# Batch 1's first heads split in the opening, loads and splits dated one by one, an output piece on ScalarE's queue

## The chip, the core and the metric

One NeuronCore of a Trainium2 chip runs the whole program. Its engines are TensorE (PE, matrix multiplies into PSUM), VectorE (DVE), ScalarE (ACT), GpSimd (POOL) and SyncE (SP, which here only issues DMAs); each works through its own list of instructions in order and waits on semaphores. 16 DMA engines move data; SP and ScalarE issue to hardware queues (q1 and q10 in the profile), GpSimd to a software queue (q0), which also casts on the way. The metric is the device time of one execution in microseconds, lower is better.

## What is computed

Clustered attention, then a two-layer network over its output:

```python
# q, k, v: 4 batches x 8 heads x 768 rows x 64, f32; centroids: 8 x 16 x 64
q_assign = argmax(einsum('bhsd,hcd->bhsc', q_n, c_n))      # nearest of 16 centroids, rows normalised
k_assign = argmax(einsum('bhsd,hcd->bhsc', k_n, c_n))
mask = q_assign[:, :, :, None] == k_assign[:, :, None, :]
scores = where(mask, q @ k.T / 8, -1e9)
attn = softmax(scores)
x = (attn @ v)  as 3072 x 512                               # rows of a batch, heads side by side
h = x @ w_in                                                # 512 x 2048
out = (h * sigmoid(h)) @ w_out                              # 2048 x 512
```

## The kernel before

**A head's inputs.** A *job* is what is loaded, split and transposed together: for batches 1 to 3 the job `h8` to `h31` of one head holds its six 128-row tiles of q and six of k (`raw`, f32). The head is *split* into two f16 parts, `hi` (L124, on ScalarE, GpSimd or DVE) and `lo` (L137, on DVE), and transposed as a whole: for `h8` and up by a DMA transposition that SP issues (`xpose`, L144), for batch 0 on PE. The transposed tile `ab` has 128 rows: the 64 of a head dimension and room for the one-hot *codes* of the nearest centroid. For these, twelve small matmuls with the centroids (`logits_n`, L178, tile `psN`), three DVE steps (sum, maximum, comparison), a matmul that turns the one-hot tile (`cd_mm`, L249), an eviction with scale (`cd_ev`, L258) and a DMA on SP into rows 64 to 79 of `ab` (L269). For batches 2 and 3 the codes go another way, by a DMA transposition and a DMA of GpSimd (L239, L243). With codes in both operands one matmul gives the score and a bonus where the clusters agree, which stands for the mask.

**Score units.** A unit is one head, one half of the query rows (384) and two key tiles: two matmuls into a double bank (`qk_mm`, L352, tile `pS`), then one exp on ScalarE (`exp`, L365, tile `P`). There are 192 units, 24 for each half of a batch. Six units later a *weighted sum* (`pv`, L373, 36 matmuls, tile `pO`) takes the P tiles of two heads, DVE normalises, and the result is transposed into `xt`, on PE or by DMA (`xn_d`, L416).

**The network.** A *first-layer piece* (`unit_a`, L437, tile `ph`) is four matmuls, a tanh on ScalarE and a gate on DVE (L452), which also frees the bank; 16 pieces make one half batch. The *second layer* (`part_b`, L464, tile `po`) takes four matmuls of w_out at a time; for most row tiles of batches 1 to 3 pairs of tiles are done by `Pair` (L519) with seven half products in place of eight, for which DVE builds sums of rows and differences of w_out (`tw_piece`, L496).

**Weights.** GpSimd issues eight pieces of w_in (`w0` to `w7`) and four of w_out (`w8` to `w11`, 512 KB each in f16) in `w_load` (L601). The last two wait for exps of units 22 and 23: a small copy out of the P tile (`pace`, L603) stands ahead of each on GpSimd.

**What sets the order.** The whole order is written into the program when it is built, nothing is decided on the chip. The opening is a list of words by hand (`plan`, L777): `r9` loads h9, `v3` casts a value tile, `qk11` and `ex11` are a unit's matmuls and exp, `e6.3` is a first-layer piece in bank 3, `w10` a weight piece; it ends after the exp of unit 26 and eight first-layer pieces. From there a planner takes over (L810 to L1230): it keeps an estimated clock for each engine, a backlog for the DMA engines (`lands`, L823), and picks step by step the next instruction for the engine that is free first. PE chooses among score units (held to a pace, L1148 to L1152), logits, weighted sums, first-layer pieces and second-layer pieces; seven-step turns (`turn`) alternate between the last two. Splits, loads and value casts of a head start at *dates*, which are unit numbers: before, a formula gives head by head the date of its split (L924), and load, values and cast stand at fixed distances from it (L927 to L931).

Buffers bind as well: raw tiles have eight places (`raw_tag`, L110), hl tiles four and later three, value loads five, P sixteen. A tile that takes a place waits on the chip until its last reader is done, whatever the planner thought.

**The end.** The last pair's last quarter product is made in two halves (`c21_last`, L593), one evicted on ScalarE, one on DVE, and both are sent by SP.

Of the kernel before, what the change touches and what calls it, by code (L numbers as in the profile page):

```python
# [34 lines left out]
def kernel(  # L35
# [74 lines left out]
    def raw_tag(n):  # L110
        return f"raw{n % 8 if n < EARLY else 5 + n % 3}"

    def load(job, eng=nc.sync):
        n = len(raws)
        raw = mp.tile([128, 12, D], f32, name="raw", tag=raw_tag(n), bufs=1)
        for dst, ap in job.srcs:
            o = raw[:, dst, :]
            if len(ap.shape) == 2:
                eng.dma_start(o.rearrange("p n d -> p (n d)"), ap)
# [245 lines left out]
    def exp(u):  # L365
        P = mp.tile([128, 2, HALF], f16, name="P", bufs=16)
        nc.scalar.activation(out=P, in_=pst.pop(u)[:, :, 0:HALF], func=AF.Exp, bias=0.0, scale=ESC)  # L367
        Ps[units[u]] = P

# [141 lines left out]
    def keep(b, n):  # L511
        if b not in cps:
            cps[b] = [mp.tile([128, HK, 128], f16, name="cp", tag=f"ab{10 + m}", bufs=1) for m in range(2)]
        nc.sync.dma_start(cps[b][n], gts[b, 0][:, n * HK : n * HK + HK, ts(NM - 1, 128)])
# [4 lines left out]
    class Pair:  # L519
# [73 lines left out]
        def c21_last(self, part):  # L593
            x = slice(part * HD // 2, part * HD // 2 + HD // 2)
            if part:
                nc.vector.tensor_copy(self.ot2[:, x], self.A[:, x])
            else:
                nc.scalar.activation(out=self.ot2[:, x], in_=self.A[:, x], func=AF.Copy, bias=0.0, scale=1.0)
            nc.sync.dma_start(self.rows()[:, 0, x], self.ot2[:, x])
# [82 lines left out]
    def first(op, n, eng, banks):  # L682
# [48 lines left out]
        elif op == "w":  # L731
            w_load(n, {10: 22, 11: 23}.get(n))
# [23 lines left out]
        elif op == "xt":  # L756
            xpose(xj)
# [29 lines left out]
        qk23 px3.3 pt1.1 pe1.D ex23 pt2.0 xc1 py3 qk24 pe2.D w7 r9 xe1.A r10 nm3 ex24 qk25 a0.1 pt3.0 w8 qk26 a1.2  # L787
        pe3.D ex25 w9 e0 e1 w10 e6.3 r11 e4.0 ex26 e2.1 e3.2 e5.3 w11 e7.0
# [21 lines left out]
    clock = dict.fromkeys(("PE", "ACT", "DVE", "POOL", "SP"), 0.0)  # L810
    lanes = {e: [] for e in clock}
# [3 lines left out]
    PACE, LEAST, GAIN = 1.40, 17, .03  # L815
    HOLD = 6
    MARGIN = 0.3
    EARLY_T = 72


    moves_end = 11
# [34 lines left out]
    code_at, tensor_todo, after_unit = {}, [], {}  # L856

    def chain(job, b):
        def split(t):
            if job.name not in loaded:  # L860
                waiting[job.name] = split
                return
            t = max(t, loaded[job.name] + 0.4)
            either(t, 0.5, 0.72, lambda e: hi(job, "act" if e == "A" else None), lambda t: add("DVE", t, 0.9, lambda: lo(job), turned, 1.5), 1.5)

        def turned(t):
            u = last_use.get(place[job.name] - 12, 0)
# [4 lines left out]
            add("SP", t, 1.5, lambda: xpose(job), lambda t: tensor_todo.append((lands(t, 2.45) + (5.0 if b == 3 else 2.2 if b == 2 else 1.8), 0.35, lambda: logits_1(job), sums)), 0.0 if b == 1 else 3.0)  # L872
# [21 lines left out]

        return split
# [4 lines left out]
    loaded, waiting, values_at = {}, {}, {}  # L900
# [4 lines left out]

    def got(job, t):
        loaded[job.name] = lands(t - 0.25, 1.31)
        if job.name in waiting:
            waiting.pop(job.name)(t)

# [5 lines left out]
    def cast(i, t):  # L916
        if i not in values_at:
            waiting[i] = lambda t: cast(i, t)
        else:
            add("POOL", max(t, values_at[i] + 0.4), 0.6, lambda: cast_v(i))  # L920

    for i in range(H, B * H):
        b, h = divmod(i, H)
        p = int((32 + 3.2 * h, 67+5.0*h, 106+5.2*h)[b - 1]) | 1  # L924
        job = jobs[i]
        if i > H + 3:
            date(max(FIRST, p - (8 + min(h, 4) if b == 1 else 16)), lambda t, job=job: add("SP", t, 1.05, lambda: load(job), lambda t: got(job, t), 3.0))  # L927
        if i >= H + 2:
            date(p - (6 if b == 1 else 9), lambda t, i=i, b=b: add("POOL", t, 0.6, lambda: load_v(i, nc.gpsimd), lambda t: got_v(i, t)) if b >= 2 else add("SP", t, 0.7, lambda: load_v(i), lambda t: got_v(i, t)))
        date(p - (3 if b == 1 else 6), chain(job, b))  # L930
        date(p, lambda t, i=i: cast(i, t))  # L931
# [27 lines left out]
    kinds = {(b, c): [0, 1, 2] for b in range(B) for c in range(2)}  # L959
    for b, c in kinds:  # L960
        if b >= 1:
            kinds[b, c] = ["p", 2]
        if b >= 2:
            kinds[b, c] = ["x", "p"] if c else ["p"]
# [41 lines left out]
    def new_pair(b, c, kind):  # L1006
        key = b, c, kind
        at.setdefault(key, {})
        t = (1 if b >= 2 else 0) if kind == "p" and c else 0
        if kind == "x":  # L1010
            r2 = (lambda h: cps[b][h]) if b in cps else tokens(b, 0, NM - 1)
            pairs[key] = Pair(kind, b, tokens(b, 1, 0), r2, NM - 1, SG[kind])
        else:
            pairs[key] = Pair(kind, b, tokens(b, c, t + 1), tokens(b, c, t), c * NM + t, SG[kind], key == LAST)
# [10 lines left out]
        if not users[kind] or "over" in at[users[kind][-1]]:  # L1025
            tell(key, "turn", 0.0)
        users[kind].append(key)
        def over(t):
            add("DVE", t + 0.2, 0.69, pr.c12, sent)
            tell(key, "over", t)  # L1030
            n = users[kind].index(key) + 1
            if n < len(users[kind]):
                tell(users[kind][n], "turn", t)
# [4 lines left out]
        qb.extend((b, c, kind, k) for k in order)  # L1038

    def unit_piece():  # L1040
# [3 lines left out]
        def gated(t):  # L1044
            gate_at[b, c, fb] = t
            for h, name in enumerate(("lo", "hi")):
                need = [gate_at.get((b, c, x)) for x in range(h * HK, h * HK + HK)]
                if h == fb // HK and None not in need:
# [3 lines left out]
                    if (b, c) in ((2, 0), (3, 0)):  # L1052
                        old = b, 1, "x"
                        at.setdefault(old, {})
                        if b == 2:
                            add("SP", t, 0.7, lambda h=h: keep(b, h), lambda t, name=name: tell(old, name + "2", lands(t, 1.0) + 1.5))
                        else:
                            tell(old, name + "2", t)

        def then(t):  # L1060
# [7 lines left out]
            elif fb == NFB - 1 and kinds[b, c][0] == 0:  # L1068
                qb.extend((b, c, t_, n) for t_ in range(NM) for n in range(4))
# [63 lines left out]
    def options(t):  # L1133
# [3 lines left out]
        if unit < NU and unit - 2 in exp_at and 6 * pv_next > unit - 11:  # L1137
            i, c, m = units[unit]
            jn = {qc[i, c][0].name, kt[i, 2 * m][0].name}
            if all(j in code_at for j in jn):  # L1140
# [7 lines left out]
                mean, least = sum(works[max(x - 1, 0) : 7]) / len(works[max(x - 1, 0) : 7]), LEAST  # L1148
                if x < 3:
                    stock, mean, least = 1.302 * len(qa) + 0.863 * len(qb) + 20.8 * (x - released), 20.8, 12  # L1150
                due = t >= scored + min(max(PACE + (mean - 20.8) / 24 + GAIN * (stock - least - mean / 24 * (24 - unit % 24)), 0.8), 2.2)
                found.append((0 if due else 6, r, 0.325, "qk"))  # L1152
        if bank_at is not None:
# [4 lines left out]
            if qa and not any(q[0] * 2 + q[1] <= qa[0][0] * 2 + qa[0][1] - 2 for q in qb):  # L1158
                r = max(x_at[qa[0][:2]], bank_at)
                found.append((2 if turn < 4 else 3, r, 0.655, "a"))  # L1160
        if qb:
# [3 lines left out]
            for k in (0, ahead):  # L1165
                if k is not None and (k or opened or len(qb) > HOLD or not a_soon):
                    r = part_ready(qb[k], bank_at)
                    if r is not None:
                        found.append((3.5 if k else 3 if turn < 4 else 2, r, (0.46 if qb[k][3] >= 40 else 0.874) if qb[k][2] in ("p", "x") else 0.863, ("b", k)))
        return found  # L1170

    def tensor_piece(o):
# [14 lines left out]
        elif what == "pv":  # L1187
            n = pv_next
            pv_next += 1
            run("PE", r, length, lambda: pv(n // 8 * H + 2 * (n % 4), n // 4 % 2), lambda t: norm_piece(n, t))  # L1190
        elif what == "a" or isinstance(what, tuple):
            turn = (turn + 1) % 7
# [67 lines left out]
```

## Time and profile before

| what | us |
|---|---|
| median of 3 runs | 302.79 |
| lowest, highest of them | 300.66, 306.08 |
| the profiled execution's own time | 300.67 |
| its span | 298.9 |
| PE busy | 289.3 |
| DVE, ACT, POOL busy | 224.0, 222.3, 73.3 |

The profile page gives the busy time of each engine in the span; the stages give the same for stretches of it; the chain of waits follows back from the last instruction what released each step; the DMA answers give, for a stretch, packets and megabytes of each queue and the share of the 16 engines that they took. A row "L362 PE MATMUL pS<-ab" is line 362 of the kernel on TensorE, the tile written and the tile read. SPq and POOLq rows are the issue of a DMA, whose landing is given beside it, in us from the start of the issue.

### The profile page before, as it was taken

The page shows a single profiled execution, that of the slowest core. Times are in us where ns is not written, and L with a number is a line of the kernel's source. Part 1 is how long each engine was busy: PE and PEld are TensorE (multiplying, and loading weights), DVE is VectorE, ACT ScalarE, POOL GpSimd, SP SyncE. Part 2 cuts the span into 40 slices and gives each one's busy share as a digit, 9 for nine tenths or more (in the row PEclk, how much of TensorE's full clock was granted, in tenths as well). Part 3 has the DMA queues.
Part 4 walks back from the last instruction along what each step waited for, and adds up shares of the span by engine and source line. Part 5 has one row for each costly group of instructions (what it writes and reads, how often), then busy time and mean ns, then how long its engine had stood idle before and what let it go on. Part 6 is the DMA issues. An engine that isn't in the chain of part 4 may idle for free.

```text
span 298.9 us, 8222 instructions
## 1 busy us (share of the span) xinstructions
PE 289.3 (97%) x3281; PEld 204.2 (68%) x3281; DVE 224.0 (75%) x474; ACT 222.3 (74%) x369; POOL 73.3 (25%) x133
## 2 busy tenths in 40 slices
PE   7899989999999999999999999999999999999994
PEld 3786756566676566667766776668667777776784
DVE  5999558787998599997789759896584535568933
ACT  4899879665896689986788769896887769854410
POOL 2894900010140052545424234232000000000000
PEclk9999999999999999999999999999999999999999
DMA  6789999999897688878899989753300021110114
GB/s 207 226 176 207 196 246 220 160 266 270 190 180 192 172 179 205 182 197 185 202 189 230 182 197 228 173 98 74 99 15 16 25 74 27 36 37 0 37 35 140
DMA packets 77364, 44.61 MB, mean 149 GB/s; under 512 B 56304, under 2 KB 73232, under 8 KB 77328
## 3 DMA queue, kind: packets, MB, share of 16 engines
q1 hardware_dynamic: 72240, 35.68, 52.2%
q0 software_dynamic: 4800, 8.13, 14.2%
q8 instruction: 25, 0.41, 0.6%
q10 hardware_dynamic: 288, 0.30, 0.3%
q14 instruction: 11, 0.09, 0.1%
HBM read 27.30 MB, written 6.29 MB: 112 GB/s over the span
## 4 chain that ended last, share of the span: by engine, by line
PE 78%; DMA 11%; ACT 5%; DVE 2%; issue 1%; POOL 1%; SPq 0%; ACTq 0%
PE ph L429 22%; PE pS L362 16%; PE po L551 15%; PE pO L379 10%; PE po L469 8%; DMA wout_s<-in_moe_w_out_dram 7%; ACT P L367 4%; PE psN L188 3%; PE wide L429 3%; DMA ab<-cd 2%; DMA raw<-in_q_dram 1%; PE wide L551 1%; DVE hl L140 1%; POOL hl L133 1%; ACT cd L265 0%
## 5 line engine op out<-in xcount | busy, mean ns | idle before, releaser
L367 ACT ACTIVATE P<-pS 128x768 f16<-128x768 f32 x192 | 155.1, 819 | 36.2 <-PE pS L362 35.7
L362 PE MATMUL pS<-ab 128*128 128x384 f16 x384 | 92.7, 326 | 0.9 <-DMA ab<-cd 0.5
L429 PE MATMUL ph<-xt,win_s 128*128 128x384 f16 x464 | 89.6, 326 | 0.9 <-DVE gt L452 0.8
L452 DVE SCALAR_TENSOR_TENSOR gt<-tn,ph 128x384 f16<-128x384 f32 x116 | 62.2, 550 | 23.2 <-ACT tn L449 22.2
L429 PEld LDWEIGHTS <-win_s 128*128 128x128 f16 x512 | 48.9, 98 | 31.7 <-issue 1.4
L449 ACT ACTIVATE tn<-ph 128x384 f32<-128x384 f32 x116 | 57.5, 502 | 7.6 <-PE ph L429 5.1
L362 PEld LDWEIGHTS <-ab 128*128 128x128 f16 x384 | 34.7, 98 | 20.5 <-issue 1.2
L379 PEld LDWEIGHTS <-P 128*128 128x128 f16 x1152 | 39.9, 97 | 4.4
L379 PE MATMUL pO<-vt,P 128*128 128x65 f16 x1152 | 41.2, 193 | 0.0
L551 PEld LDWEIGHTS <-gt 128*128 128x128 f16 x312 | 29.5, 98 | 6.2 <-DVE gt L533 0.7
L140 DVE SCALAR_TENSOR_TENSOR hl<-raw,hl 128x768 f16<-128x768 f32 (+3 forms) x35 | 32.5, 930 | 1.2 <-ACT hl L131 0.6
L469 PE MATMUL po<-wout_s,gt 128*128 128x512 f16 x128 | 32.8, 379 | 0.2 <-DMA wout_s<-in_moe_w_out_dram 0.2
L303 POOL CAST vt<-vn 128x384 f16<-128x384 f32 x32 | 19.3, 604 | 48.1 <-DMA vn<-in_v_dram 40.3
L551 PE MATMUL po<-wout_s,gt 128*128 128x256 f16 x168 | 21.3, 273 | 0.1
L245 POOL DMA_DIRECT2D ab<-cdt x16 | 8.9, 559 | 50.0 <-PE pS L362 20.4
L188 PEld LDWEIGHTS <-ab 128*128 128x128 f16 x458 | 17.4, 97 | 4.2 <-DVE ab L174 0.3
L469 PEld LDWEIGHTS <-gt 128*128 128x128 f16 x128 | 12.0, 98 | 10.8 <-issue 0.4
L389 DVE RECIPROCAL zr<-pO 128x6 f32<-128x6 f32 x32 | 6.2, 194 | 17.3 <-PE pO L379 17.0
L391 DVE TENSOR_TENSOR xn<-pO,zr 128x384 f16<-128x384 f32 x32 | 17.8, 557 | 1.1
L188 PE MATMUL psN<-stk,ab 128*128 128x32 f16 (+1 forms) x458 | 18.6, 188 | 0.0
L200 DVE TENSOR_REDUCE L<-psN 128x192 f32<-128x384 f32 (+1 forms) x27 | 14.8, 549 | 3.5 <-PE psN L188 3.4
L232 POOL TENSOR_SCALAR od<-od 128x96 f16<-128x96 f16 x16 | 8.8, 548 | 33.1 <-DVE od L225 32.6
(106 smaller groups left out, 276.8 us busy)
## 6 DMA issues: line engine op xcount, KB each, us to landing
raw<-in_k_dram SPq DMA_DIRECT2D x31, 192.0 KB, 4.0
out_dram<-ot SPq DMA_DIRECT2D x23, 256.0 KB, 2.3
raw<-in_q_dram SPq DMA_DIRECT2D x24, 192.0 KB, 3.9
vn<-in_v_dram SPq DMA_DIRECT2D x16, 192.0 KB, 4.4
vn<-in_v_dram POOLq DMA_DIRECT2D x16, 192.0 KB, 4.0
win_s<-in_moe_w_in_dram POOLq DMA_DIRECT2D x8, 256.0 KB, 7.1
wout_s<-in_moe_w_out_dram POOLq DMA_DIRECT2D x4, 512.0 KB, 18.5
raw<-in_q_dram SPq DMA_DIRECT2D x2, 384.0 KB, 4.3
```

The costliest lines, as they stand in the source:

```text
L140: nc.vector.scalar_tensor_tensor(out=hl[:, s, 1, :], in0=raws[job.name][:, s, :], scalar=QS, in1=hl[:, s, 0, :], op0=ALU.mult, op1=ALU.sub ...
L188: nc.tensor.matmul(L[:, n % g, :, n // g], ab[:, i, :], stk[:, job.groups[i // 3][0], x : x + w], start=(x == 0), stop=(x + w == 2 * HC),)
L303: nc.gpsimd.tensor_copy(vt[:, :, 0:D], vns.pop(i))
L362: nc.tensor.matmul(pS[:, e, 0:HALF], abs_[kj.name][:, kn, :], rhs, start=True, stop=True)
L367: nc.scalar.activation(out=P, in_=pst.pop(u)[:, :, 0:HALF], func=AF.Exp, bias=0.0, scale=ESC)
L379: nc.tensor.matmul(o[:, (2 * t + h) * VW : (2 * t + h + 1) * VW], Ps[i + h, c, j // 2][:, j % 2, ts(t, 128)], vtb[(i + h) % 13][:, j, 0:VW ...
L391: nc.vector.tensor_tensor(out=xn, in0=ov[:, :, 0:D], in1=zr.unsqueeze(2).to_broadcast([128, 2 * NM, D]), op=ALU.mult)
L429: nc.tensor.matmul(ph[:, 0:HALF], win_s[:, r, ts(fb, 128)], xts[b, c][:, r, :], start=(r == 0), stop=(r == NR - 1))
L449: nc.scalar.activation(out=tn, in_=ph[:, 0:HALF], func=AF.Tanh, bias=0.0, scale=1.0)
L452: nc.vector.scalar_tensor_tensor(out=gt[:, fb, :], in0=tn, scalar=1.0, in1=ph[:, 0:HALF], op0=ALU.add, op1=ALU.mult)
L469: nc.tensor.matmul(po, gts[b, c][:, fc, ts(t, 128)], wout_s[:, fc, :], start=(fc == 0), stop=(fc == NFB - 1))
L551: nc.tensor.matmul(o, l[:, f, :], x[:, x0 : x0 + w], start=(f == 0 and k in begins), stop=(f == HK - 1), skip_group_check=True)
```

## The change

- **Opening.** hi of h8 on ScalarE behind x1's code eviction (`hi8.A`); the load of h11 moves ahead by some words, and behind it lo and the transposition of h8 (`lo8 ht8`); at the list's end hi, lo and transposition of h9 (`hi9.D lo9 ht9`). Their logits are then put on PE by the planner from fixed times (`turned_at`). The pace copies of w10 and w11 wait for units 24 and 25.
- **Dates.** `SPLIT` gives the split of each head of batches 1 to 3 its unit, `AHEAD`, `VALUES` and `CAST` the distances of load, value load and cast by batch. The planner now lets a load, a value load, a cast and a split wait in its own clock until the buffer that they take is free (`raw_free`, `value_free`, `cast`, `split`), and second-layer pieces of the first half batch wait for `weights_at`.
- **Limits.** Pace, the stock of network work kept, the length of a turn and the lead of units over weighted sums have new values; P has 12 buffers; heads 16 and 17 of the order use raw5 to raw7, so that the w_out differences start at unit 58 in place of 72.
- **End.** The first of the two last output pieces is issued by ScalarE.
- `CROSS`, `PAIRS`, `room` and `kept` write the choice of pairs in another way; the kinds of second-layer pieces come out the same.

```diff
     def raw_tag(n):
-        return f"raw{n % 8 if n < EARLY else 5 + n % 3}"
+        return f"raw{n % 8 if n < 2 * H else 5 + n % 3}"
...
-        P = mp.tile([128, 2, HALF], f16, name="P", bufs=16)
+        P = mp.tile([128, 2, HALF], f16, name="P", bufs=12)
...
-            nc.sync.dma_start(self.rows()[:, 0, x], self.ot2[:, x])
+            (nc.sync if part else nc.scalar).dma_start(self.rows()[:, 0, x], self.ot2[:, x])
...
-            w_load(n, {10: 22, 11: 23}.get(n))
+            w_load(n, {10: 24, 11: 25}.get(n))
...
-        elif op == "xt":
-            xpose(xj)
+        elif op == "ht":
+            xpose(job)
...
-        qk23 px3.3 pt1.1 pe1.D ex23 pt2.0 xc1 py3 qk24 pe2.D w7 r9 xe1.A r10 nm3 ex24 qk25 a0.1 pt3.0 w8 qk26 a1.2
-        pe3.D ex25 w9 e0 e1 w10 e6.3 r11 e4.0 ex26 e2.1 e3.2 e5.3 w11 e7.0
+        qk23 px3.3 pt1.1 pe1.D ex23 pt2.0 xc1 py3 qk24 pe2.D w7 r9 xe1.A hi8.A r10 nm3 ex24 qk25 a0.1 pt3.0 w8 qk26 a1.2
+        pe3.D r11 lo8 ht8 ex25 w9 e0 e1 w10 e6.3 e4.0 ex26 e2.1 e3.2 e5.3 w11 e7.0
+        hi9.D lo9 ht9
...
     clock = dict.fromkeys(("PE", "ACT", "DVE", "POOL", "SP"), 0.0)
+    clock["DVE"] = 2.0
-    PACE, LEAST, GAIN = 1.40, 17, .03
-    HOLD = 6
-    MARGIN = 0.3
-    EARLY_T = 72
-    moves_end = 11
+    PACE, LEAST, LESS, GAIN = 0.95, 25, 7, 0.03
+    HOLD, ROUND, SIDE, LEAD = -23, 7, 3, 11
+    MARGIN = 1.0
+    EARLY_T = 58
+    moves_end = 13.0
...
+    turned_at = {"h8": 5.0, "h9": 9.5}
+    weights_at = (3.0, 6.0, 9.5, 13.0)
     def chain(job, b):
         def split(t):
+            old = int(job.name[1:]) - (3 if int(job.name[1:]) >= H + 8 else 4)
+            if old >= H + 2 and old not in turn_at:
+                after_turn[old] = split
+                return
             if job.name not in loaded:
                 waiting[job.name] = split
                 return
-            t = max(t, loaded[job.name] + 0.4)
+            t = max(t, loaded[job.name] + 0.4, turn_at.get(old, 0.0) + 0.3)
...
+        if job.name in turned_at:
+            return lambda t: turning(turned_at[job.name])
         return split
...
+    SPLIT = [27, 27, 36, 42, 45, 47, 52, 55, 66, 67, 70, 75, 84, 86, 87, 88, 91, 107, 111, 114, 118, 121, 126, 129]
+    AHEAD, VALUES, CAST = [18, 4, 0], [3, 11, 11], [8, 9, 16]
     for i in range(H, B * H):
         b, h = divmod(i, H)
-        p = int((32 + 3.2 * h, 67+5.0*h, 106+5.2*h)[b - 1]) | 1
+        p = SPLIT[i - H]
...
-                if x < 3:
-                    stock, mean, least = 1.302 * len(qa) + 0.863 * len(qb) + 20.8 * (x - released), 20.8, 12
+                mean, least = sum(works[max(x - 1, 0) : 7]) / len(works[max(x - 1, 0) : 7]), LEAST if x > 2 else LESS
...
-            need = [gate_at.get((b, c, fb)) for fb in range(4 * n, 4 * n + 4)] + ([bank_at] if n == 0 else [])
+            need = [weights_at[n]] + [gate_at.get((b, c, fb)) for fb in range(4 * n, 4 * n + 4)] + ([bank_at] if n == 0 else [])
```

More of the change, by code (lines that the diff above doesn't have):

```diff
@@ L899 @@
             code_at[job.name] = 4.0 if job.name == "x1" else 0.0
-    loaded, waiting, values_at = {}, {}, {}
+    loaded, waiting, values_at, pv_at, after_pv = {}, {}, {}, {}, {}
+    for n in range(4):
+        pv_at[n] = 0.0
     for n in range(8, 12):
@@ L904, with raw_free @@
         values_at[n] = 0.0
+    split_at, after_split = {i: 0.0 for i in range(H + 2)}, {}
+    def raw_free(i, t):
+        old = max((m for m in range(i) if raw_tag(m + 2) == raw_tag(i + 2)), default=0)
+        if old >= H and old not in split_at:
+            after_split[old] = lambda t: raw_free(i, t)
+        else:
+            add("SP", max(t, split_at.get(old, 0.0) + 0.06), 1.05, lambda: load(jobs[i]), lambda t: got(jobs[i], t), 3.0)
     def got(job, t):
@@ L909, in got, with value_free @@
             waiting.pop(job.name)(t)
+    cast_at, after_cast = {i: 0.0 for i in range(H)}, {}
+    def value_free(i, t):
+        if i - 5 not in cast_at:
+            after_cast[i - 5] = lambda t: value_free(i, t)
+            return
+        t = max(t, cast_at[i - 5] + 0.06)
+        if i >= 2 * H:
+            add("POOL", t, 0.6, lambda: load_v(i, nc.gpsimd), lambda t: got_v(i, t))
+        else:
+            add("SP", t, 0.7, lambda: load_v(i), lambda t: got_v(i, t))
     def got_v(i, t):
@@ L1051, in gated @@
                             tell(key, name + x, max(need))
[L1052 to L1058, printed above, removed]
+                    if c == 0 and b in CROSS:
+                        kept(b, h, t)
         def then(t):
```

91 lines of the change are left out of this document (61 added, 30 removed).

## The prediction

> **What bounds the kernel now.** I read the page's busy times first, then the stages, then the chain of waits.
>
> ```profile
> span 298.9 us, 8222 instructions
> PE 289.3 (97%) x3281; PEld 204.2 (68%) x3281; DVE 224.0 (75%) x474; ACT 222.3 (74%) x369; POOL 73.3 (25%) x133
> ```
>
> TensorE is busy 97% of the span. The stages say where the other 3% lies.
>
> ```profile
> 42.00:49.00 7.00, 6.16 (x68) 4.05 (x67) 4.98 (x11) 6.00 (x11) 0.00 (x0) 1.00 1.20 244
> 49.00:62.00 13.00, 12.75 (x114) 7.55 (x113) 9.78 (x20) 9.32 (x14) 1.02 (x2) 1.00 1.24 200
> 62.00:100.00 38.00, 37.91 (x442) 24.68 (x440) 31.57 (x66) 27.82 (x45) 5.51 (x11) 1.00 0.94 209
> 100.00:200.00 100.00, 99.99 (x1144) 69.22 (x1141) 86.85 (x173) 81.72 (x133) 37.24 (x70) 1.00 0.89 190
> 200.00:263.00 63.00, 62.75 (x692) 46.34 (x691) 35.24 (x71) 51.11 (x85) 3.30 (x8) 1.00 0.18 45
> 263.00:294.90 31.90, 31.83 (x284) 24.75 (x280) 23.04 (x46) 11.32 (x27) 0.00 (x0) 1.00 0.12 40
> ```
>
> The first busy column is PE, the last three are the granted clock, the share of the 16 DMA engines and GB/s. From 62 to 294.9 us PE idles 0.09 + 0.01 + 0.25 + 0.07 = 0.42 us, from 42 to 62 it idles 1.09 us. The rest of the idle time is in the opening before 42 us, whose PE order the change keeps up to unit 26, and in the tail after the last matmul. So no gain of 2% (6 us) is there to be had behind 42 us; a new wait of PE, on the other hand, is paid in full, since nothing later has room to absorb it. The 1.24 says where a wait can come from: from 42 to 62 us the DMA engines are full. The chain names it too.
>
> ```profile
> 35.93 22.30 DMA wout_s<-in_moe_w_out_dram
> 58.27 1.02 PE po L469 x4
> 60.48 0.33 PE pS L362 x2
> 60.81 0.35 PE psN L188 x12
> 80.36 0.65 PE ph L429 x4
> PE po L469 <- DMA wout_s<-in_moe_w_out_dram: 0.2, 1, 0.2
> ```
>
> The last w_out piece is 22.3 us under way and PE waits 0.2 us for it (the list of waits). The other rows are sizes for later: a score unit, a head's logits, a piece of the first layer.
>
> **The change, part by part.** The instruction orders of the two kernels hold the same PE work; what moves is when. Before, h8 (batch 1's first head) is split on DVE and transposed by SP from 48.1, and its twelve logits come behind the 42nd score unit. In the changed order hi of h8 is on ScalarE, lo on DVE, its transposition follows h11's load on SP, and its logits stand on PE right behind the 33rd score unit. h9 follows four units later, behind the 37th.
>
> *Splits.* hi of h8 goes behind x1's code eviction and ahead of an exp.
>
> ```profile
> 35.47 0.38 ACT L265 ACTIVATE cd<-psN 96x256 f16<-96x256 f32 x1
> 36.42 1.51 ACT L367 ACTIVATE P<-pS 128x768 f16<-128x768 f32 x2 [0.57 <-PE pS L362]
> L131 ACT ACTIVATE hl<-raw 128x768 f16<-128x768 f32 x1 | 0.9, 867 | 0.0
> 41.52 2.07 DVE L452 SCALAR_TENSOR_TENSOR gt<-tn,ph 128x384 f16<-128x384 f32 x4 [0.53 <-ACT tn L449]
> 45.02 0.56 DVE L452 SCALAR_TENSOR_TENSOR gt<-tn,ph 128x384 f16<-128x384 f32 x1 [1.42 <-ACT tn L449]
> L140 DVE SCALAR_TENSOR_TENSOR hl<-raw,hl 128x768 f16<-128x768 f32 x26 | 25.1, 967 | 0.3
> L135 DVE TENSOR_SCALAR hl<-raw 128x768 f16<-128x768 f32 x23 | 13.4, 582 | 0.0
> ```
>
> ScalarE is free at 35.85; 0.87 of hi ends at 36.72, so the exp that began at 36.42 is 0.3 us late, and the next score unit waits for that exp's bank: **+0.3**. lo of h8 (0.97) fits on DVE before the first gate. hi and lo of h9 (0.58 + 0.97) begin behind the eighth gate at 43.59 and end at 45.14, 0.1 behind where the next gate began: the 1.42 of idle time there covers them, cost nothing; without that cover it would be 1.5.
>
> *The transpositions against w_out.* SP issues h8's transposition behind h11's load (issued last at 38.2), and a queue's transfers land in the order of issue, as those of 62.3 and 63.5 further below do, at 66.8 and 68.1. So it lands after that load.
>
> ```profile
> L119 SPq DMA_DIRECT2D raw<-in_k_dram x1: 479/479/479, 38.2 to 38.2; - x1
> DMA to landing us min/median/max: 10.2/10.2/10.2
> 48.64 0.49 PE L362 MATMUL pS<-ab 128*128 128x384 f16 x2
> 48.96 0.49 PE L429 MATMUL ph<-xt,win_s 128*128 128x384 f16 x2
> L149 SPq DMA_TRANSPOSE ab<-hl x1: 4196/4196/4196, 48.1 to 48.1; - x1
> DMA to landing us min/median/max: 11.0/11.0/11.0
> ```
>
> The load lands at 38.2 + 10.2 = 48.4. PE ends the 33rd score unit at 48.96, with the 0.3 late at 49.3, and then wants h8. How long the transposition takes is the price that decides. The nearest row is h8's own: 11.0 us from issue, 4.2 of them the issue, so 6.8 beside w_out. The other end is h11's, with w_out gone: it landed at 63.5 + 4.6 = 68.1, 1.3 behind the load before it (62.3 + 4.5 = 66.8).
>
> ```profile
> L149 SPq DMA_TRANSPOSE ab<-hl x1: 2439/2439/2439, 63.5 to 63.5; - x1
> DMA to landing us min/median/max: 4.6/4.6/4.6
> L298 SPq DMA_DIRECT2D vn<-in_v_dram x1: 996/996/996, 62.3 to 62.3; - x1
> DMA to landing us min/median/max: 4.5/4.5/4.5
> ```
>
> Between them the queues themselves: the answers for 52.3 to 54.5 us, when w_out and h8's transposition ran side by side, and for 54.5 to 58.3.
>
> ```profile
> q0 software_dynamic: 245, 0.24, 64.7%
> q1 hardware_dynamic: 610, 0.16, 62.4%
> ...
> q1 hardware_dynamic: 911, 0.23, 115.9%
> q0 software_dynamic: 84, 0.08, 12.5%
> ```
>
> q0 carries the weights, q1 SP's transfers. The transposition is 610 + 911, some 1,520 packets; side by side it moved 610 in 2.2 us, 277 a us, so 5.5 us for one. I take this rate, since w_out has most of its last two pieces to go at 48.4, and it lies nearer to 6.8. h8 lands at 48.4 + 5.5 = 53.9: PE waits 53.9 - 49.3 = **+4.6** (bounds 48.4 + 1.3 = 49.7, a wait of 0.4, and 48.4 + 6.8 = 55.2, a wait of 5.9). h9's transposition is behind it in the queue: at 59.4. Between the two sets of logits PE has one set (0.35 us), four score units (0.33 each), four first-layer pieces (0.65 each) and five small matmuls (0.3, an estimate from the 0.29 of two in a row below), 4.5 us, so it arrives at 49.3 + 4.6 + 4.5 = 58.4: **+1.0** (bounds none and 2.2, for 6.8 each).
>
> By the Trainium skill ("DMA: Bandwidth & Descriptors", section "Queues, rings and completion order") each DMA engine goes round-robin between the queues it has work for, packet by packet. The time shares above, 64.7% and 62.4%, agree; but the transposition ran at a quarter, not half, of what it does alone, so I keep the row. What an even split would give is the second rival.
>
> *w_out.* The pace copies of the last two pieces wait for exps 24 and 25 instead of 22 and 23, some 2.5 us later; behind them on GpSimd are only casts of values that batch 1 needs far later. The pieces ahead fill q0 meanwhile, so their landing doesn't move by that. It moves by what the transpositions take from q0, but the first second-layer piece now stands two score units and a whole weighted-sum group later, and the waits above delay it more: the 0.2 goes, and with it what pipelining hides of the same wait, 0.2 more at most: **-0.4** (bounds 0.2 and 0.4).
>
> *Tail.* Before, SP issues the last two pieces in a row.
>
> ```profile
> 295.18 0.29 DVE L596 COPY ot<-po 128x128 f32<-128x128 f32 x1 [0.72 <-ACT ot L598]
> 295.38 0.89 SPq L599 DMA_DIRECT2D out_dram<-ot  x2
> ```
>
> With the first on ScalarE's queue, idle by then, the second goes out when its copy ends at 295.47, not in the second half of those 0.89 us, at 295.8: **-0.4**, all of it on the path (nothing if the landing were what's late).
>
> *The planner.* New dates and limits reorder units, loads and splits; the listed numbers change no instruction count on PE. Twelve P buffers for sixteen cost nothing as long as each weighted sum stands on PE ahead of the score unit twelve behind, which the new lead of 11 sees to. The w_out differences on DVE come 14 units earlier, into a stretch where it is busy 31.57 of 38 us: covered, or gates would be late. Batch 1's first score units come earlier in PE's order, and the time from a head's code matmul to its first use shrinks: for h10 I count 6.9 us on PE, where before its code matmul at 71.42 was followed by the landing of its codes 8.4 later, at 76.9 + 3.0 = 79.9.
>
> ```profile
> 71.42 0.29 PE L254 MATMUL psC<-ident,om 128*96 128x128 f16 x2
> L269 SPq DMA_DIRECT2D ab<-cd x1: 757/757/757, 76.9 to 76.9; - x1
> DMA to landing us min/median/max: 3.0/3.0/3.0
> ```
>
> Most of that, 5.5 us, is the way to the issue, behind a queue that the changed order relieves by two transpositions; so I take 0, bounds 0 and 1.5.
>
> Sum against the profiled execution's 300.67 (span 298.9): 0.3 + 4.6 + 1.0 - 0.4 - 0.4 = +5.1, **305.8**. The median before is 302.79, of 300.66 to 306.08, so single runs scatter by more than this sum's steps.
>
> **Rivals.** *No wait:* the transposition passes w_out at its pace alone and lands at 49.7. For it: it is only 0.2 MB, and 1.3 us is measured. Against it: all of 54.5 to 58.3, where 84 packets of w_out were enough to hold it at 240 a us. It would leave 0.3 + 0.4 - 0.8: 300.6, not slower. It decides if h8 lands before 50.1. *An even split:* 2.6 us each, h8 at 51.0, a wait of 1.7, none for h9: 301.5 with the 0.3 and the 0.8. *The slow rate throughout:* 5.9 + 2.2 + 0.3 - 0.8 = +7.6, 308.3. *Codes late as well:* the forecast and 1.5, 307.3.
>
> **How the numbers follow.** Forecast 0.42 (its own range 303 to 308), no wait 0.22, even split 0.16, slow rate 0.12, late codes 0.08. The range takes in all but the ends of these, 299.5 to 309. A measurement here can tell about 2% from no change, 6 us: none of the cases is that much faster (0.02 for what I don't see); slower by it are the slow rate, half of the late codes and a fifth of the forecast, 0.24; the rest is 0.74.
>
> **What would show it.** A wait of PE at the logits of h8 near 49 us, put down to the transposition, of 3.5 to 6 us, and a smaller one at h9's; the transposition issued near 39 and landed near 54; the wait for w_out gone; the last output issued 0.4 us sooner after the last matmul; PE full behind 65 us. No wait at h8's logits, or one elsewhere of over 2 us, makes this wrong.

## The result and the profile after

| what | before | after |
|---|---|---|
| median, us | 302.43 | 315.83 |
| lowest to highest of 4 runs | 300.66 to 306.08 | 314.02 to 317.27 |
| profiled execution | 300.67 | 317.27 |
| its span | 298.9 | 315.3 |

The ratio is 1.046, with a 95% interval of 1.037 to 1.055: slower, by 13.4 us. The forecast was 305.8, its range ended at 309.0, and only 0.24 of its chances were for slower; 0.74 stood for a time that can't be told from no change. The sum had the right sign and the right place. Its largest term, 4.6 us, was about half of the 8.6 measured, and two losses were not in it: the half clock behind the wait, and waits that the planner's part brings.

The head of the page of the changed kernel:

```profile
span 315.3 us, 8257 instructions
...
PE 291.5 (92%) x3281; PEld 205.3 (65%) x3281; DVE 223.2 (71%) x472; ACT 222.6 (71%) x371; POOL 71.8 (23%) x133
```

TensorE has the same 3281 matmuls, and is busy 2.2 us longer than the 289.3 of before, though nothing was added for it. The stages say where both come from (stretch, its length, busy time of PE, PEld, DVE, ACT and POOL, the granted clock, the share of the DMA engines, GB/s):

```profile
49.00:65.00 16.00, 7.39 (x54) 4.27 (x51) 4.29 (x11) 4.79 (x8) 0.51 (x1) 0.68 0.98 178
65.00:170.00 105.00, 105.00 (x1185) 70.04 (x1183) 88.95 (x180) 80.84 (x129) 29.24 (x57) 1.00 0.85 184
170.00:190.00 20.00, 16.10 (x216) 11.95 (x215) 14.33 (x28) 13.89 (x24) 3.48 (x8) 1.00 0.92 178
...
265.00:300.00 35.00, 32.49 (x266) 23.10 (x263) 23.42 (x45) 14.76 (x33) 0.00 (x0) 1.00 0.09 31
```

Three stretches lose time: 8.6 us of idle PE between 49 and 65, where the granted clock is also down to 0.68 on average; 3.9 between 170 and 190; 2.5 between 265 and 300. The list of waits of the changed kernel (who waits for whom, us in all, times, the longest) has the largest at its head:

```profile
PE psN L187 <- DMA ab<-hl: 8.6, 1, 8.6
PE pS L361 <- ACT P L366: 3.2, 2, 2.2
```

**Between 49 and 65.** PE in the timeline (start, duration, line, count, and in brackets the idle time ahead and who ended it):

```profile
49.22 0.49 PE L361 MATMUL pS<-ab 128*128 128x384 f16 x2
58.31 0.82 PE L187 MATMUL psN<-stk,ab 128*128 128x32 f16 x12 [8.61 <-DMA ab<-hl]
58.95 1.47 PE L428 MATMUL ph<-xt,win_s 128*128 128x384 f16 x4
...
64.36 0.81 PE L428 MATMUL ph<-xt,win_s 128*128 128x384 f16 x4
```

PE came to h8's logits at 49.71, 0.4 behind where the forecast put it, and got them at 58.31. Behind the wait the same four matmuls of a first-layer piece take 1.47 us, where from 64.36 on they take 0.81. That is the granted clock: a mean of 0.68 over 16 us is 2 × 0.32 × 16 = 10.2 us at half clock. Some 5 us of these lay behind the wait; at 0.66 lost of each 1.47 they cost about 2.3 us, which is the longer busy time of the page.

The DMA answers of the changed kernel for 39 to 40, 40 to 41, 49 to 53 and 58 to 60 us (in the queue rows: packets, MB, time taken as a share of 16 engines; in the issue rows KB and us from issue to landing):

```profile
wout_s<-in_moe_w_out_dram POOLq DMA_DIRECT2D x1, 512.0 KB, 18.8
...
ab<-hl SPq DMA_TRANSPOSE x1, 18.2
...
q0 software_dynamic: 617, 0.60, 90.0%
q1 hardware_dynamic: 617, 0.16, 31.3%
...
q1 hardware_dynamic: 1330, 0.64, 117.0%
```

The last w_out piece was issued at 39.09 and landed 18.8 later, at 57.9; h8's transposition, issued at 40.02, landed 18.2 later, at 58.3. In the 4 us in which both queues had work all the time each moved 617 packets, 154 a us: one for one, w_out's of 1 KB, the transposition's of 256 B. With w_out gone, from 58 to 60, SP's queue moved 1330 packets, 665 a us, the last of them larger ones of loads.

**Between 170 and 190.** The timeline of DVE, ACT and PE there, one after the other:

```profile
178.90 0.56 DVE L134 TENSOR_SCALAR hl<-raw 128x768 f16<-128x768 f32 x1 [2.78 <-DMA raw<-in_k_dram]
...
186.58 0.84 ACT L130 ACTIVATE hl<-raw 128x768 f16<-128x768 f32 x1 [3.40 <-DMA raw<-in_k_dram]
...
180.97 1.03 PE L550 MATMUL po<-wout_s,gt 128*128 128x256 f16 x8 [1.68 <-DVE gt L451]
...
188.17 0.48 PE L361 MATMUL pS<-ab 128*128 128x384 f16 x2 [2.22 <-ACT P L366]
```

Two splits of batch 3's heads stand on their engine ahead of their load's landing: DVE waits 2.78 us, with gates behind it that second-layer matmuls want; ScalarE waits 3.40, with exps behind it whose banks the next score unit wants. PE pays 1.68 + 2.22 = 3.9.

**Behind 265.** PE again:

```profile
272.04 0.81 PE L428 MATMUL wide<-xt,win_s 128*128 128x384 f16 x4 [1.22 <-DVE gt L451]
292.79 0.81 PE L428 MATMUL wide<-xt,win_s 128*128 128x384 f16 x4 [0.60 <-ACT tn L448]
294.64 1.03 PE L550 MATMUL po<-wout_s,gt 128*128 128x256 f16 x8 [0.40 <-DVE ot L576]
298.80 1.03 PE L550 MATMUL wide<-wout_s,gt 128*128 128x256 f16 x8 [0.29 <-DVE gt L451]
```

Here banks are late, 1.22 + 0.60 + 0.40 + 0.29 = 2.5. When the last score unit is done PE has 29 first-layer pieces left, 21 in the kernel before (counted in the two traces); they follow each other with little between them, faster than tanh and gate give a bank back. That the number of pieces is the cause is not shown: e_ahead, further below, has 28 of them and idles 1.8 us there, in other places.

So 8.6 + 2.3 + 3.9 + 2.5 = 17.3. The opening is 0.6 later, the 0.5 that PE idled before in 49 to 62 and 200 to 263 is gone, and the tail is 0.75 shorter: 16.65, against 16.4 between the spans. The profiles are of the longest execution of the changed kernel and of nearly the shortest before; between the medians there are 13.4, so some of these waits are smaller in other executions.

### The profile page after: what moved, and what is told of

Its sections match the earlier page's. It is cut to its first block, busy times and chain, and to the rows that moved or that the text cites. A ratio compares the mean times of both kernels' runs of the same rounds, so it can differ in the third digit from the quotient of the medians.

```text
span 315.3 us, 8257 instructions
## 1 busy us (share of the span) xinstructions
PE 291.5 (92%) x3281; PEld 205.3 (65%) x3281; DVE 223.2 (71%) x472; ACT 222.6 (71%) x371; POOL 71.8 (23%) x133
## 3 DMA queue, kind: packets, MB, share of 16 engines
q0 software_dynamic: 4800, 8.13, 13.7%
## 4 chain that ended last, share of the span: by engine, by line
PE 78%; DMA 12%; ACT 4%; SPq 2%; DVE 2%; issue 1%; POOL 1%; ACTq 0%; POOLq 0%; DVEq 0%
PE ph L428 21%; PE pS L361 17%; PE po L550 11%; PE pO L378 10%; PE po L468 8%; DMA ab<-hl 6%; PE wide L428 3%; PE wide L550 3%; PE psN L187 3%; DMA raw<-in_k_dram 3%; DMA ab<-cd 2%; SPq L118 2%; ACT P L366 2%; DMA raw<-in_q_dram 1%; DVE gt L451 1%
## 5 line engine op out<-in xcount | busy, mean ns | idle before, releaser
L366 ACT ACTIVATE P<-pS 128x768 f16<-128x768 f32 x192 | 156.9, 827 | 29.4 <-PE pS L361 27.4
L361 PE MATMUL pS<-ab 128*128 128x384 f16 x384 | 94.0, 328 | 4.3 <-ACT P L366 3.2
L428 PE MATMUL ph<-xt,win_s 128*128 128x384 f16 x444 | 88.5, 330 | 0.8 <-DVE gt L451 0.8
L451 DVE SCALAR_TENSOR_TENSOR gt<-tn,ph 128x384 f16<-128x384 f32 x111 | 59.9, 549 | 25.6 <-ACT tn L448 24.9
L428 PEld LDWEIGHTS <-win_s 128*128 128x128 f16 x512 | 49.5, 99 | 34.0 <-issue 4.4
L448 ACT ACTIVATE tn<-ph 128x384 f32<-128x384 f32 x111 | 56.0, 511 | 19.0 <-PE ph L428 18.5
L550 PE MATMUL po<-wout_s,gt 128*128 128x256 f16 x160 | 20.6, 273 | 2.1 <-DVE gt L451 1.7
L448 ACT ACTIVATE tn<-wide 128x384 f32<-128x384 f32 x17 | 8.0, 492 | 14.4 <-PE wide L428 10.8
## 6 DMA issues: line engine op xcount, KB each, us to landing
wout_s<-in_moe_w_out_dram POOLq DMA_DIRECT2D x4, 512.0 KB, 17.3
```

Of the source, the lines that this page charges most:

```text
L361: nc.tensor.matmul(pS[:, e, 0:HALF], abs_[kj.name][:, kn, :], rhs, start=True, stop=True)
L428: nc.tensor.matmul(ph[:, 0:HALF], win_s[:, r, ts(fb, 128)], xts[b, c][:, r, :], start=(r == 0), stop=(r == NR - 1))
L448: nc.scalar.activation(out=tn, in_=ph[:, 0:HALF], func=AF.Tanh, bias=0.0, scale=1.0)
L451: nc.vector.scalar_tensor_tensor(out=gt[:, fb, :], in0=tn, scalar=1.0, in1=ph[:, 0:HALF], op0=ALU.add, op1=ALU.mult)
L550: nc.tensor.matmul(o, l[:, f, :], x[:, x0 : x0 + w], start=(f == 0 and k in begins), stop=(f == HK - 1), skip_group_check=True)
```

## The experiments

The theory behind the first ones: h8's transposition can't land before w_out is done, so its logits must not stand on PE before that; and the half clock is a consequence of the wait. The rivals: the time is lost in the planner's new dates, or SP's queue is what is late. In all of them the line numbers of waits are those of the changed kernel, unless said.

**Logits behind the landing (e_late).**

```diff
-    turned_at = {"h8": 5.0, "h9": 9.5}
-    weights_at = (3.0, 6.0, 9.5, 13.0)
+    turned_at = {"h8": 16.0, "h9": 17.5}
+    weights_at = (3.0, 7.0, 11.5, 14.6)
```

> The logits of h8 and h9 are dated 16.0 and 17.5 on the planner's clock instead of 5.0 and 9.5 (and the weight dates set to the landings seen: 3, 7, 11.5, 14.6); splits and transpositions stay in the opening. Theory: PE's 8.6 us wait at h8's logits and the some 2.3 us of half clock behind it are all that the early logits cost, and both go: about 306 us, 1.2% above before, with the waits near 180 us and 270 to 298 us left. Rival: the wait only moves, to the codes of batch 1's first units, and the time stays above 311 us.

Measured: 305.9 (304.56 to 311.33), ratio to before 1.011 (1.001 to 1.021). The stage of the wait in e_late, and a later stretch of it:

```profile
49.00:62.00 13.00, 13.00 (x148) 8.33 (x146) 8.21 (x17) 10.02 (x15) 0.38 (x1) 1.00 1.25 232
...
91.40:95.00 3.60, 3.16 (x21) 1.87 (x22) 1.52 (x4) 0.49 (x1) 0.00 (x0) 0.53 1.04 253
```

PE is full from 49 to 62 at full clock, while the DMA engines are as full as ever: 10 us come back by moving two sets of twelve small matmuls and, behind them, the first second-layer pieces. (The profiled execution took 309.37. It has a wait of 2.6 us at another head's logits, up to 91.8, and the half clock of the second row behind it; its mean granted clock is 0.993, that of the three shorter runs, the median among them, 1.00, so the half clock at least is not in the median.) Some 3 to 4 us stay.

**w_out without its last two pieces (e_noload).** They are replaced by zeros on GpSimd, so half of the second layer's sum is left out.

```diff
         if after is not None:
             nc.gpsimd.tensor_copy(pace, Ps[units[after]][0:1, 0, 0:1])
+            nc.gpsimd.memset(wout_s[:, 4 * (n - 8) : 4 * (n - 8) + 4, :], 0.0)
+            return
```

> The last two pieces of w_out are not loaded, their half of w_out is set to zero by GpSimd instead, so half of the second layer's sum is left out. Theory: SP's transposition takes turns packet by packet with w_out, and can't end before w_out ends; with w_out ending near 50 us h8 lands at 50 to 52 us, PE waits under 2.5 us, and no half clock follows. Rival: the transposition is slow by itself behind the loads (its issue alone took 8.1 us); it lands near 57 to 58 us and PE waits over 6 us.

Measured, once: 311.22. The last piece that is still loaded lands at 51.5, h8's transposition at 53.9, 4.4 sooner than in the changed kernel. PE in the timeline of e_noload:

```profile
53.94 0.82 PE L187 MATMUL psN<-stk,ab 128*128 128x32 f16 x12 [4.00 <-DMA ab<-hl]
```

The stage around it:

```profile
49.00:61.00 12.00, 8.00 (x63) 4.67 (x60) 4.48 (x11) 5.08 (x9) 0.53 (x1) 0.72 0.75 158
```

The landing follows the end of w_out, though here by 2.4 us and not by 0.4. The DMA answer of e_noload for 52.3 to 53.5 us shows why:

```profile
DMA packets 69, 0.02 MB, mean 15 GB/s; under 512 B 69, under 2 KB 69, under 8 KB 69
```

With no other queue at work the engines all but stopped there for over a us. They had done so from 47.6 to 49.5 too (148 packets), when w_out was still under way, so it ended later than the expectation assumed; the wait shrank to 4.0 and did not go. The half clock came all the same (2 × 0.28 × 12 = 6.7 us).

**The wait filled with matmuls (e_junk).** Thirty matmuls of 512 columns on zeros stand ahead of h8's logits.

```diff
     def logits_1(job):
+        if job.name == "h8":
+            psNs[job.name] = bank("psN")
+            for _ in range(30):
+                nc.tensor.matmul(psNs[job.name], zz[:, 0:128], zz, start=True, stop=True)
```

> 30 matmuls of 512 columns on zeros stand ahead of h8's logits, 6.5 us at full clock, in the bank that the logits then overwrite. Theory: the half clock from 58 to 64 us comes from PE being idle; with the wait cut to some 2 us the clock stays at 1.0 and the piece from 58.3 to 64.3 us (end of the wait to the code matmul of h8) shrinks from 5.9 to about 3.6 us. Rival: the clock falls for another reason, and that piece keeps its 5.9 us.

Measured, once: 318.78. From the list of waits of e_junk:

```profile
PE psN L187 <- DMA ab<-hl: 2.1, 1, 2.1
```

The stretches behind this wait and behind one of 3.2 us for an exp, near 188:

```profile
58.74:65.00 6.26, 6.25 (x44) 3.91 (x45) 3.53 (x8) 3.55 (x7) 0.51 (x1) 0.73 0.59 186
...
188.40:192.10 3.70, 3.70 (x47) 2.98 (x44) 2.85 (x5) 1.84 (x3) 2.08 (x5) 0.54 0.82 162
```

The expectation that the half clock would go was wrong: 2.1 us of idle time were left, and 2 × 0.27 × 6.26 = 3.4 us at half clock followed them, against 10.2. The second place shows the same, 2 × 0.46 × 3.7 = 3.4. The time shows nothing gained, so what the half clock costs is taken from the timeline alone.

**The opening alone, in the kernel before (b_open).** The list of the opening, the pace copies and the fixed times of h8's and h9's logits, on the planner of before (which also dates their splits at unit 27 and starts its clock of DVE at 2.0, as the change does); its core:

```diff
-        qk23 px3.3 pt1.1 pe1.D ex23 pt2.0 xc1 py3 qk24 pe2.D w7 r9 xe1.A r10 nm3 ex24 qk25 a0.1 pt3.0 w8 qk26 a1.2
-        pe3.D ex25 w9 e0 e1 w10 e6.3 r11 e4.0 ex26 e2.1 e3.2 e5.3 w11 e7.0
+        qk23 px3.3 pt1.1 pe1.D ex23 pt2.0 xc1 py3 qk24 pe2.D w7 r9 xe1.A hi8.A r10 nm3 ex24 qk25 a0.1 pt3.0 w8 qk26 a1.2
+        pe3.D r11 lo8 ht8 ex25 w9 e0 e1 w10 e6.3 e4.0 ex26 e2.1 e3.2 e5.3 w11 e7.0
+        hi9.D lo9 ht9
...
+        if job.name in ("h8", "h9"):
+            return lambda t: tensor_todo.append(({"h8": 5.0, "h9": 9.5}[job.name], 0.35, lambda: logits_1(job), sums))
```

> The kernel before with the opening of the change alone: the words of the list, the pace copies at units 24 and 25, and the logits of h8 and h9 at 5.0 and 9.5 on the planner's clock. Theory: the opening is the cause of most of the loss; PE waits 8 to 9 us at h8's logits, some 2.3 us more go to the half clock, and the time is 312 to 313 us against some 302. Rival: the opening needs the new planner to do harm, or only the dates do; the time stays under 308 us.

Measured: 312.61 (311.53 to 313.27), ratio 1.037 (1.031 to 1.042). The wait at h8's logits is 9.8 us here, the 18 us of the first of these stages less its 8.19 of busy PE:

```profile
49.00:67.00 18.00, 8.19 (x61) 4.65 (x58) 4.77 (x12) 5.29 (x10) 1.01 (x2) 0.62 0.90 153
67.00:200.00 133.00, 133.00 (x1508) 89.81 (x1505) 111.59 (x221) 103.43 (x164) 37.85 (x73) 1.00 0.93 188
```

The wait and the half clock (2 × 0.38 × 18 = 13.7 us of it) come with the opening alone, and the 133 us behind are without a gap. The opening by itself costs most of what the whole change does.

**All but the opening (e_words).** The changed kernel with the opening, the pace copies and h8's and h9's way to their logits as before; the edit undoes the lines of the opening shown above, and

```diff
-    turned_at = {"h8": 5.0, "h9": 9.5}
+    turned_at = {}
```

> The changed kernel with the opening's list, the pace copies and h8's and h9's way to their logits as before, so only the planner's dates and limits, the buffers and the end are changed. Theory: the opening alone cost 10.2 us in the kernel before, and the rest of the change has a cost of its own, the 3.7 us that were left when h8's logits were moved behind the landing: 305 to 307.5, no wait of PE at logits over 1.5 us before 65 us, and waits of 1 to 3 us between 170 and 190 and again in the last 40 us. Rival: the planner's part is neutral, as the prediction had it, and those 3.7 us came from the early splits and transpositions of h8 and h9 too: 301 to 303.5.

Measured: 309.56 (307.05 to 310.3), ratio 1.027 (1.023 to 1.031). More than the theory expected, and in another place. The stages of e_words:

```profile
100.00:170.00 70.00, 65.94 (x770) 44.60 (x768) 55.43 (x114) 53.70 (x87) 21.50 (x44) 1.00 0.94 190
170.00:190.00 20.00, 19.67 (x251) 14.59 (x249) 17.73 (x35) 15.83 (x26) 3.99 (x8) 1.00 0.93 207
...
263.00:304.50 41.50, 38.71 (x304) 28.78 (x303) 27.64 (x52) 15.86 (x36) 0.00 (x0) 1.00 0.13 45
```

PE in its timeline, where 100 to 170 loses time:

```profile
107.43 0.48 PE L361 MATMUL pS<-ab 128*128 128x384 f16 x2 [0.63 <-ACT P L366]
...
138.92 0.52 PE L187 MATMUL psN<-stk,ab 128*128 128x32 f16 x12 [1.20 <-DMA ab<-hl]
```

The planner's part is not neutral: 4.1 us are idle between 100 and 170, in small waits for exps, codes, banks and one transposition, and 2.8 behind 263, with the same 1.22, 0.59, 0.40 and 0.30 at the end as in the changed kernel. But its price hangs on the order that it falls into: the two waits near 180 of the changed kernel are not there, and the two parts do not add. Alone they cost 3.7% and 2.7%, together 4.6%.

**Batch 3's loads sooner (e_ahead).**

```diff
-    AHEAD, VALUES, CAST = [18, 4, 0], [3, 11, 11], [8, 9, 16]
+    AHEAD, VALUES, CAST = [18, 4, 8], [3, 11, 11], [8, 9, 16]
```

> Batch 3's loads are dated 8 units ahead of their split instead of 0, nothing else. Theory: the two waits near 179 and 186 us (1.7 and 2.2 us) are splits that stand on DVE and ScalarE ahead of gates and exps and wait for a raw tile that SP issued too late; they go, and the time falls by about 4 us, to 312 us. Rival: the loads meet the transpositions of batch 2, other waits take their place, and the time stays at 315 to 316 us.

Measured: 316.05 (313.95 to 318.59), ratio 1.048 (1.039 to 1.057): no faster than the changed kernel. The stages of e_ahead:

```profile
170.00:190.00 20.00, 20.00 (x217) 14.44 (x215) 15.51 (x30) 15.21 (x24) 6.19 (x13) 1.00 0.96 187
265.00:308.00 43.00, 41.21 (x353) 30.94 (x351) 28.54 (x55) 15.80 (x35) 0.00 (x0) 1.00 0.12 43
```

In this order the load date caused the waits near 180: the timeline names the loads, and with the earlier date the waits are gone. (They are gone in e_words too, with the old date, so the order counts as well.) That this is worth time is not shown: the median stands where it was. Its profiled execution, 313.95, is the lowest of its runs, with a span of 312.0, 3.3 below that of the changed kernel's profile, which was the longest of its own; the runs of both scatter by 3 to 5 us, so what the edit is worth within that stays open.

**Both mends, and the old limits (e_fix, f_pace).** e_fix is e_late with this load date; f_pace adds

```diff
-    PACE, LEAST, LESS, GAIN = 0.95, 25, 7, 0.03
+    PACE, LEAST, LESS, GAIN = 1.40, 17, 7, 0.03
```

> Late logits of h8 and h9 and batch 3's loads 8 units ahead, together. Theory: each takes away its own waits, so what is left against before are waits of some 2.5 us for banks behind the last score unit and singles of 1 to 3 us from run to run: 302 to 304 us, ratio to before 1.00 to 1.01. Rival: the rest of the change (pace, dates) costs as much by itself, and the ratio stays at 1.011 or above, as with the late logits alone.

> As the run before it in this list, and the pace and stock of before (1.40, 17) in place of 0.95 and 25, by which 21 first-layer pieces instead of 28 stand behind the last score unit on PE. Theory: PE's waits for banks and tanh behind the last score unit come from that many first-layer pieces in a row there; they fall under 0.8 us in all, and the time to 301 to 303 us. Rival: slower score units at the pace of before bring other waits, and the time is as in the run before.

Measured: e_fix 306.11 (303.82 to 310.97), ratio 1.010 (1.002 to 1.018); f_pace 307.85 (306.7 to 309.38), 1.022 (1.016 to 1.028). Both lie above the times expected of them, and neither is better than e_late. From the list of waits of f_pace:

```profile
PE pS L361 <- ACT P L366: 3.4, 8, 1.0
```

21 first-layer pieces are left behind the last score unit, as before, and the waits for banks at the end are mostly gone; but eight short waits of score units for exps take their place. The old values, on the new dates, do not give the old order back.

**The last piece but one on ScalarE's queue, in the kernel before (b_tail).**

```diff
-            nc.sync.dma_start(self.rows()[:, 0, x], self.ot2[:, x])
+            (nc.sync if part else nc.scalar).dma_start(self.rows()[:, 0, x], self.ot2[:, x])
```

> The kernel before with the last but one output piece issued by ScalarE, nothing else. Theory: the last issue on SP starts some 0.4 us sooner behind the last matmul than before (1.0 us behind its end before, 0.65 after), and the span ends that much sooner behind it. Rival: the landing of the other piece is what is late, and the distance from the last matmul to the end of the span stays at 4.0 us.

Measured, once: 300.22. The last issues in the timeline of b_tail, and below them those of the changed kernel:

```profile
294.44 0.43 SPq L580 DMA_DIRECT2D out_dram<-ot  x1
...
294.75 0.35 ACTq L599 DMA_DIRECT2D out_dram<-ot  x1
...
295.07 0.33 SPq L599 DMA_DIRECT2D out_dram<-ot  x1
```

```profile
310.72 0.33 SPq L579 DMA_DIRECT2D out_dram<-ot  x1
...
312.69 0.33 SPq L598 DMA_DIRECT2D out_dram<-ot  x1
```

In b_tail the last issue is 0.4 us nearer to PE's end, and the time from there to the span's end stays 4.04 (4.06 before). The last landing, 297.0, stands 0.4 behind that of the 256 KB piece issued at 294.44, which lands at 296.6: it seems to wait for the transfer ahead, not for its issue. So the queue alone gives nothing. In the changed kernel that large piece goes out 1.3 us before PE ends, and the tail is 3.31; but in e_ahead it goes out 1.8 us before, with the same queues, and the tail is 3.97. Where the 0.75 come from stays open.

## Why the prediction was wrong

- **The frame held.** PE had nothing to spare behind 42 us, so each new wait was paid in full, and the place named for the new wait, h8's logits, was right: PE at 49.7 (49.3 said), h11's load ahead in the queue landing at 48.8 (48.4).
- **The step that failed: "side by side it moved 610 in 2.2 us, 277 a us, so 5.5 us for one".** Beside w_out the transposition got one packet for each of w_out's, 154 a us, and its end came with w_out's: +8.6 for +4.6, and beyond the bound of 5.9. The 277 were read in a stretch in which w_out's packets ran out, 245 in the first 2.2 us and 84 in the next 3.8. The DMA answers of the kernel before for 52.3 to 53.5 and for 53.5 to 54.5 take the 2.2 us apart:

```profile
q0 software_dynamic: 174, 0.17, 86.6%
q1 hardware_dynamic: 216, 0.06, 35.1%
...
q1 hardware_dynamic: 394, 0.10, 95.2%
q0 software_dynamic: 71, 0.06, 38.4%
```

  At first the count is near one for one, 174 to 216; only then does SP's queue get more. (That some of the 16 engines had no w_out packets left by then is inferred; the trace does not name the engines.) The numbers for a better sum stood in the prediction itself: w_out had "most of its last two pieces to go", 1 MB or about 1,000 packets of 1 KB, against some 1,520 of the transposition. At one for one w_out's end, 58.27 in the chain of waits, comes with a third of the transposition still to move, and h8 lands behind it. By the Trainium skill ("DMA: Bandwidth & Descriptors", section "Queues, rings and completion order") an engine goes round-robin between its queues, packet by packet; the trace agrees, 617 to 617. The prediction weighed this rule, set it aside for the row, and where it priced it as a rival took half of the time for half of the packets: 2.6 us, the far side of the truth. Turns by packets give little to a queue whose packets are a quarter of the size, and they lead to the end of the other queue's work. One thing they don't explain: from 54.5 to 58.3 in the kernel before the transposition moved only 240 packets a us beside 84 of w_out. By its share of time, 115.9%, a packet took 77 ns there, against 32 ns (31.3%) beside w_out in the changed kernel. What held it then stays open.
- **h9's +1.0 did not come.** It landed at 59.6 (59.4 said), but PE, held by h8, came later still.
- **Not in the sum at all: the half clock behind the wait, about 2.3 us.** Of what PE does after a wait the sum held only its end.
- **The planner, taken at 0, with PE "full behind 65 us".** 3.9 + 2.5 were lost there, and e_words shows that the part costs on its own, +8 us with the opening of before. The wait of 2.22 near 188 is the "one elsewhere of over 2 us" that the prediction named as its sign of being wrong. The 1.5 kept as a bound was for codes, which were not what was late: loads that a split waits for, and banks at the end. The prediction's reason, that instruction counts on PE stay, says nothing about order, and the order of loads against splits could be read in the instruction streams.
- **The splits.** hi of h8 cost next to nothing. ScalarE in the timeline of the changed kernel:

```profile
36.00 0.38 ACT L264 ACTIVATE cd<-psN 96x256 f16<-96x256 f32 x1
...
37.02 1.49 ACT L366 ACTIVATE P<-pS 128x768 f16<-128x768 f32 x2
```

  The exp behind it began 0.6 later than before, at 37.02 for 36.42, but the code eviction ahead of it was 0.53 later already, at 36.00 for 35.47. The +0.3 is at most 0.1.
- **w_out's wait went, as said**; the tail gained 0.75 where 0.4 were said, but not for the reason given: in b_tail the other queue alone gave nothing.
- **The rivals.** "The slow rate throughout", 308.3, was the nearest: the sign and the place were right, and even its rate of 6.8 us for a transposition was too fast. Two slips beside the sum: the even split's terms give 301.9, not 301.5, and a transposition of some 1,520 packets of 256 B is 0.39 MB (0.16 + 0.23 in the rows shown), not 0.2.

What stays open: the 3 to 4 us (1.1% and 1.0%) that e_late and e_fix still lose. They are spread over waits mostly under 2 us that move from one version to the next, and no edit tried here removed them together.

## What to carry to other kernels

Price a transfer that runs beside another queue by counting packets of both, not by a rate from a stretch in which the other queue was running out; a transposition with small packets landed here when its neighbour was done. Put nothing on a full engine's list before such a landing: moving two heads' logits behind it brought 10 us back here (e_late), and the wait cost its length and a stretch at half clock behind it. And when a hand-tuned set of dates is replaced, read each split against its own load's landing, since no count of instructions shows a load that comes late.

## What the runs showed of the hardware

**The clock falls after waits of 2 to 10 us, in steps of 3.4 us.** From the rows above: 10.2 us at half clock with a wait of 8.6, 13.7 with 9.8, 6.7 with 4.0, 3.4 with 3.2, 2.6 and 2.1 (the last behind matmuls on zeros); that is three, four, two and one times 3.4. None came with the waits of 2.22 and 1.68 near 180, where the granted clock is 1.00. By the Trainium skill ("TensorE: Matmul & The Clock Gate", Part 1) activity is counted in free-running windows of 3.4 us, with half rate after at least one idle window and full rate after a busy one. The step agrees; but waits of 2.1, 2.6 and 3.2 us, too short to hold a whole window, were followed by half clock too, and one of 2.2 was not. The traces resolve this when PE's idle time is counted by stretches of 3.41 us that end where the clock changes. Two such stretches of the changed kernel, then two of b_open:

```profile
186.33:189.74 3.41, 1.57 (x44) 1.44 (x44) 2.17 (x5) 3.16 (x5) 0.96 (x3) 1.00 0.84 225
189.74:193.15 3.41, 3.41 (x35) 2.41 (x32) 2.65 (x6) 2.57 (x5) 1.31 (x3) 1.00 1.06 190
...
48.01:51.42 3.41, 1.46 (x39) 1.07 (x36) 1.38 (x4) 2.09 (x4) 0.00 (x0) 1.00 1.12 169
51.42:54.84 3.42, 0.00 (x0) 0.00 (x0) 0.00 (x0) 0.00 (x0) 0.00 (x0) 0.50 1.33 146
```

The wait of 2.22 falls into two stretches and leaves 3.41 - 1.57 = 1.84 us idle in the second: no half clock. In b_open 1.95 us are idle in one: half clock follows. In the eleven traces of this case each such stretch at full clock, up to the last matmul, with 1.95 us or more idle was followed by one at half clock, and none with 1.84 or less. So what counted was how much of one stretch was idle, a little over half of it, and a wait of 2.1 us was enough where it fell into one.

**A transposition's issue took longer where its queue was held up.** SP's row in the timeline of the changed kernel:

```profile
40.02 16.39 SPq L148 DMA_TRANSPOSE ab<-hl  x2
```

Two issues took 8.2 us each, against 4.2 and 2.4 for the two of before that the prediction quotes; the loads for the next heads, behind them on SP, were issued from 56.5 on.

**Stops of the DMA engines.** From 53.2 to 54.2 us, the changed kernel, in the DMA answer:

```profile
DMA packets 96, 0.06 MB, mean 58 GB/s; under 512 B 52, under 2 KB 96, under 8 KB 96
```

96 packets in that us, where 617 + 617 in 4 us are 308. It held h8 back by about 0.7 us. The two stops of e_noload, above, are of the same kind. What they are, no run here tells.
